# A value product with 7 block products for 8, and the norm moved to ScalarE, in a fused attention and gated-unit kernel

## Chip, cores, metric

One core of one Trainium2 chip. The time is device microseconds (us) of one execution on that core.

## The reference

```python
kv  = einsum('bhsd,bhse->bhde', k, v)          # b=8, h=8, s=576, d=64
o   = einsum('bhsd,bhde->bhse', q, kv)
o   = o / sqrt(mean(o*o, axis=-1) + 1e-6) * g_norm
x   = o as (8, 576, 512)                       # heads side by side
pre = sum over 5 taps of conv_w[tap] * x moved by 4 - tap tokens (zeros before the start)
out = ((sigmoid(pre) * (x @ w_val)) @ w_out)   # w_val, w_out 512 x 512
```

The three weights come as float64 and are narrowed by the kernel; the rest is float32.

## The kernel before

A batch is 576 tokens: four chunks of 128 and one of 64. For each chunk, TensorE makes `raw` (the attention output), then the norm follows, x is turned, gates and value product are made from it, and the output product closes the batch. The parts that matter here (cut):

```python
BANKS = {"kv": 1, "raw": 2, "tp": 2, "mm": 3}                 # PSUM banks by use
xTs = [const.tile([P, NK, SX], FP32, name=f"xT{i}") for i in range(3)]

def square(b, c):                      # ScalarE, all 8 heads of a chunk at once
    nc.scalar.activation(out=sq[:, 0:n, 0:D], in_=raw..., func=AF.Square)
def sums(b, c):                        # VectorE: the 8 head sums at once
    nc.vector.reduce_sum(out=ss[:, 0:n], in_=st["sq", b, c][:, 0:n], axis=AX.X)
def powers(b, c):                      # GpSimd: ss ** -0.5
def normalise(b, c):                   # VectorE: raw * rt, all 8 heads at once
    nc.vector.tensor_tensor(out=x..., in0=raw..., in1=rt....broadcast_to((P, n, D)), op=ALU.mult)

def val_product(b, jt, n):             # TensorE: 4 products of 128 rows for each block of 288 tokens
    for kc in range(NK):
        nc.tensor.matmul(val[:], wval[:, kc, jt * P:(jt + 1) * P],
            xTs[b % 3][:, kc, HALO + n * SV:HALO + (n + 1) * SV], start=(kc == 0), stop=(kc == NK - 1))
def keep_val(b, jt, n):                # ScalarE: one copy out of PSUM
    nc.scalar.copy(out=gv[:, jt, first:first + SV], in_=st["val", b, jt, n][:])
```

The output product already uses the 2x2 scheme with 7 block products (`fast_product`), with 2 copies and 5 additions for each pair of chunks (`fast_keep`).

**How the order comes about.** Each engine executes its own list of instructions in one fixed order (in the traces of the change and of the six experiments that keep its order, PE's 2113 records come in the same sequence, whatever their times), and the program makes that order itself: every step is entered with the engine, an *assumed duration*, a *wanted time*, what it needs, and the buffers it takes and frees; a planner then lists the steps by the earliest start it computes. A table of shifts, fitted by whoever wrote the kernel, corrects the wanted times.

```python
class Planner:
    HOP = 0.24                         # us from one engine to another
    def add(self, engine, time, want, fn, *args, needs=(), gives=(), takes=(), frees=(), ...):
        want += SHIFTS.get(fn.__name__, {}).get(which..., 0.0)
    def order(self):                   # always the step with the least (start, want)
...
plan.add("ACT", 0.52 * part, t + 1.0, square, b, c, needs=[("raw", b, c)], gives=[("sq", key)], ...)
plan.add("DVE", 0.6 * part, t + 4.2, normalise, b, c, needs=[("raw", b, c), ("rt", key)], ...)
```

## Time and profile before

| | before |
|---|---|
| time, median of 3 runs | 342.95 us (339.98 to 343.47) |
| span of the profiled run, granted clock | 339.4 us, 0.995 |
| TensorE (PE) / VectorE (DVE) / ScalarE (ACT) busy | 315.1 / 270.4 / 139.4 us |
| PE idle: first 82 us, 82 to 320, after 320 | 15.9, 3.2, 5.3 us |

The prediction below shows the page of this kernel and its main groups. Here is the busy time by stretch of the kernel before, in two stretches; the columns are the stretch, its length, PE, PE weight loads, DVE, ACT and GpSimd (busy us and instructions), granted clock, DMA share, GB/s:

```profile
0.00:82.00 82.00, 66.08 (x658) 54.84 (x659) 62.04 (x134) 52.52 (x113) 31.81 (x30) 0.98 1.00 274
82.00:320.00 238.00, 234.85 (x1450) 189.67 (x1449) 203.97 (x353) 85.21 (x177) 108.22 (x148) 1.00 0.51 133
```

In the middle PE is busy 234.85 of 238 us, while ACT is busy 85.21.

"Busy" counts the time covered by matmul records, and a record reaches past the point where the next one could start (407 ns mean against a spacing of 242.5), so a late start of less than about 0.16 us is hidden in it. I therefore also took **pace and loss** from the starts of the matmul records in the trace: for each kind of record (same product and size) the 30th percentile of the distance to the next start is its pace (242 ns for 288 columns, 216 for 256); the sum of the paces is the time that PE needs, and whatever the distances exceed it by is loss: waits, dependence stalls and stretches at half clock. Before: pace 274.3 us, loss 53.4 us (31.6 in the first 82 us, 21.3 from 82 to 320, 0.5 after), of which a part are small products that sometimes start nearly together.

### The profile page before, as it was taken

To read this page: it belongs to the slowest core of one execution; us is meant where nothing else is said; L and a number is where in the kernel's file an instruction comes from. 1 tells how busy PE (TensorE), PEld (TensorE's weight loads), DVE (VectorE), ACT (ScalarE), POOL (GpSimd) and SP (SyncE) were. 2 spreads that over 40 slices of the span, in tenths; PEclk is the share of its full clock that TensorE was granted. 3 is DMA by queue.
4 is the path that set the end of the run, shared out by engine and by line. 5 is a ranking of instruction groups with operands and counts; after the bars stand their busy time and mean duration, and the time that the engine had idled before them with its cause. 6 is when DMAs were issued, how large, how long until landed. Compare 5 with 4: busy or idle time off the path is not lost.

```text
span 339.4 us, 6185 instructions
## 1 busy us (share of the span) xinstructions
PE 315.1 (93%) x2161; PEld 254.7 (75%) x2161; DVE 270.4 (80%) x496; ACT 139.4 (41%) x293; POOL 140.0 (41%) x178
## 2 busy tenths in 40 slices
PE   0858999999999999999999999999999999999794
PEld 0747777878778877788778888778878876878681
DVE  4607999989999799896999899789956997297620
ACT  5528983873134253235134533172215322353010
POOL 3007314784356642683365585601717458000000
PEclk9998999999999999999999999999999999999999
DMA  6999979997077979787793165365333215220223
GB/s 165 287 329 306 320 219 299 250 315 168 3 178 196 244 233 280 187 236 207 206 256 86 32 154 157 71 182 144 79 89 85 64 31 129 58 63 2 62 62 93
DMA packets 46012, 55.35 MB, mean 163 GB/s; under 512 B 15754, under 2 KB 36254, under 8 KB 45982
## 3 DMA queue, kind: packets, MB, share of 16 engines
q1 hardware_dynamic: 42750, 48.67, 52.7%
q0 software_dynamic: 3072, 6.30, 8.3%
q8 instruction: 17, 0.28, 0.4%
q14 instruction: 13, 0.11, 0.1%
q10 hardware_dynamic: 160, 0.00, 0.0%
HBM read 39.21 MB, written 9.44 MB: 143 GB/s over the span
## 4 chain that ended last, share of the span: by engine, by line
PE 77%; DVE 8%; DMA 8%; ACT 3%; SPq 2%; issue 1%; POOL 1%; DVEq 0%
PE val L567 34%; PE ac L639 15%; PE b L639 11%; PE raw L469 8%; DMA q<-in_q_dram 5%; PE kv L392 4%; DMA k<-in_k_dram 2%; PE out L587 2%; PE qTps L430 2%; DVE gate L555 2%; PE xTps L515 1%; DVE sums L622 1%; DVE gv L580 1%; DMA out_dram<-ot 1%; DVE ss L491 1%
## 5 line engine op out<-in xcount | busy, mean ns | idle before, releaser
L567 PE MATMUL val<-xT,wval 128*128 128x288 f32 x512 | 129.5, 407 | 0.5 <-ACT gv L576 0.5
L567 PEld LDWEIGHTS val<-xT,wval 128*128 128x128 f32 x512 | 95.8, 190 | 26.9 <-issue 1.5
L497 POOL TENSOR_TENSOR rt<-ss,mhalf 128x8 f32<-128x8 f32 (+1 forms) x40 | 66.5, 1668 | 114.7 <-DVE ss L491 114.4
L555 DVE SCALAR_TENSOR_TENSOR gate<-xT,cwT,gate 128x576 f32<-128x576 f32 x128 | 97.4, 808 | 1.9 <-ACT gate L549 1.9
L538 POOL DMA_DIRECT2D xT<-y x96 | 52.9, 557 | 18.1 <-issue 6.5
L576 ACT COPY gv<-val 128x288 f32<-128x288 f32 x64 | 25.3, 395 | 69.3 <-PE val L567 69.1
L469 PEld LDWEIGHTS raw<-kvbd,qT 128*128 128x128 f32 (+1 forms) x320 | 36.8, 187 | 5.0 <-issue 1.9
L469 PE MATMUL raw<-kvbd,qT 128*128 128x128 f32 (+1 forms) x320 | 40.1, 286 | 0.0
L491 DVE TENSOR_REDUCE ss<-sq 128x8 f32<-128x520 f32 (+1 forms) x40 | 25.0, 630 | 17.5 <-ACT sq L483 17.5
L639 PE MATMUL b<-wsum,sums 128*128 128x256 f32 x128 | 33.6, 385 | 3.1 <-DVE sums L622 2.7
L639 PE MATMUL ac<-wout,gv 128*128 128x256 f32 x128 | 33.6, 385 | 0.2 <-DVE ot L662 0.2
L483 ACT ACTIVATE sq<-raw 128x512 f32<-128x512 f32 (+1 forms) x40 | 22.0, 553 | 24.0 <-PE raw L469 23.9
L639 PEld LDWEIGHTS b<-wsum,sums 128*128 128x128 f32 x128 | 23.1, 190 | 7.7 <-DVE sums L622 2.3
L504 DVE TENSOR_TENSOR x<-raw,rt 128x512 f32<-128x512 f32 (+1 forms) x40 | 24.9, 627 | 3.0 <-POOL rt L497 2.7
L639 PEld LDWEIGHTS ac<-wout,gv 128*128 128x128 f32 x128 | 23.4, 190 | 4.7 <-DVE ot L662 1.1
L562 ACT ACTIVATE gate<-gate 128x576 f32<-128x576 f32 x32 | 21.6, 684 | 11.8 <-DVE gate L555 11.4
L580 DVE TENSOR_TENSOR gv<-gv,gate 128x576 f32<-128x576 f32 x32 | 24.0, 749 | 2.6 <-ACT gv L576 1.9
L545 POOL COPY xT<-xT 128x124 f32<-128x124 f32 x32 | 18.7, 622 | 13.5 <-DMA xT<-y 13.5
L549 ACT ACTIVATE gate<-xT,cwT 128x576 f32<-128x576 f32 x32 | 22.2, 765 | 2.3 <-DMA xT<-y 2.2
L392 PEld LDWEIGHTS kv<-v,k 128*64 128x64 f32 x512 | 17.8, 138 | 6.5 <-issue 5.7
L392 PE MATMUL kv<-v,k 128*64 128x64 f32 x512 | 20.4, 225 | 1.9 <-DMA v<-in_v_dram 1.9
L655 ACT COPY ot<-ac 128x256 f32<-128x256 f32 x16 | 6.0, 372 | 35.6 <-PE ac L639 30.1
(78 smaller groups left out, 335.1 us busy)
## 6 DMA issues: line engine op xcount, KB each, us to landing
q<-in_q_dram SPq DMA_DIRECT2D x96, 140.0 KB, 4.6
out_dram<-ot SPq DMA_DIRECT2D x144, 64.0 KB, 1.8
k<-in_k_dram SPq DMA_DIRECT2D x16, 512.0 KB, 8.0
v<-in_v_dram SPq DMA_DIRECT2D x16, 512.0 KB, 7.3
xT<-y POOLq DMA_DIRECT2D x96, 64.0 KB, 2.7
w_wval<-in_moe_w_val_dram SPq DMA_DIRECT2D x4, 512.0 KB, 7.0
q<-in_q_dram SPq DMA_DIRECT2D x4, 512.0 KB, 8.7
w_wout<-in_moe_w_out_dram SPq DMA_DIRECT2D x4, 512.0 KB, 8.6
```

The source lines that it names most:

```text
L392: nc.tensor.matmul(kvp[r * D:(r + 1) * D, hp, :], st["k", b, half][:, h, j, :] if j < NJ else kl[:, 2 * hp + r, :], st["v", b, half][:, h, ...
L469: nc.tensor.matmul(raw[row * m:(row + 1) * m, col * P:(col + 1) * P], st["qT", b][:, hp, c * P:c * P + m], kv_bd[b % 2][:, hp, :], start=T ...
L491: nc.vector.reduce_sum(out=ss[:, 0:n], in_=st["sq", b, c][:, 0:n], axis=AX.X)
L497: nc.gpsimd.tensor_tensor(out=rt[:, 0:n], in0=st["ss", b, c][:, 0:n], in1=mhalf[:, 0:n], op=ALU.pow)
L504: nc.vector.tensor_tensor(out=x[:, 0:n * D].rearrange("p (h e) -> p h e", h=n), in0=st["raw", b, c][:, 0:n * D].rearrange("p (h e) -> p h ...
L538: nc.gpsimd.dma_start(out=xTs[b % 3][i * TB:(i + 1) * TB, :, first:first + P], in_=y[a * TB:(a + 1) * TB, i])
L549: nc.scalar.activation(out=gate[:], in_=xTs[b % 3][:, jt, HALO:SX], func=AF.Copy, scale=cwT[:, K - 1, jt:jt + 1])
L555: nc.vector.scalar_tensor_tensor(out=gate[:], in0=xTs[b % 3][:, jt, tap * TB:tap * TB + S], scalar=cwT[:, tap, jt:jt + 1], in1=gate[:], op ...
L567: nc.tensor.matmul(val[:], wval[:, kc, jt * P:(jt + 1) * P], xTs[b % 3][:, kc, HALO + n * SV:HALO + (n + 1) * SV], start=(kc == 0), stop=( ...
L576: nc.scalar.copy(out=gv[:, jt, first:first + SV], in_=st["val", b, jt, n][:])
L580: nc.vector.tensor_tensor(out=both, in0=both, in1=st["gate", b, jt][:], op=ALU.mult)
L639: nc.tensor.matmul(st[bank, i, p], tokens()[:, k], weights_[:, k], start=(n < 2 and k == 0), stop=(k == NK // 2 - 1), skip_group_check=True)
```

## The change

Its intent: PE sets the time, so the value product of batches 2 to 7 is made with 7 block products instead of 8. The sums and differences that this needs cost VectorE time, so the norm of those batches goes from VectorE to ScalarE, head by head. The output product's additions fall from 5 to 3. The order is replanned with a new table of shifts. The core of the diff (cut at "..."):

```diff
+    ACT_NORM = range(2, B)
+    ACT_SUMS = range(2, B)
+    FAST_VAL = range(2, B)
+    GATES = 3                                              # 4 gate tiles before
-    BANKS = {"kv": 1, "raw": 2, "tp": 2, "mm": 3}
+    BANKS = {"kv": 1, "raw": 2, "tp": 1, "mm": 4}
-    xTs = [... for i in range(3)]
+    xTs = [... for i in range(2)]
+    junk = const.tile([P, D], FP32, name="junk")
...
     def square(b, c):
+        if b in ACT_SUMS:
+            for h in range(n):
+                nc.scalar.activation(
+                    out=junk[:], in_=st["raw", b, c][:, h * D:(h + 1) * D], func=AF.Square,
+                    accum_out=ss[:, h:h + 1])
+            return
...
     def normalise(b, c):
+        if b in ACT_NORM:
+            for h in range(n):
+                cols = slice(h * D, (h + 1) * D)
+                nc.scalar.activation(out=x[:, cols], in_=st["raw", b, c][:, cols], func=AF.Copy,
+                    scale=st["rt", b, c][:, h:h + 1])
+            return
...
+    def val_fast(b, mj, n):            # n = 0..6, banks a, c, a, b, a, c, a
+        for k in range(NK // 2):
+            nc.tensor.matmul(st[bank, "val", b, mj][:], weights_[:, k], tokens()[:, k], ...)
+    def val_keep(b, mj, n):            # copies on ScalarE for n = 0, 1, 2, 6, additions on VectorE for 3, 4, 5
...
     def fast_keep(i, p, n):            # output product: 4 copies + 3 additions, 2 + 5 before
...
-            plan.add("ACT", 0.52 * part, t + 1.0, square, ...)
+                plan.add("ACT", 1.4 * part, t + 1.0, square, ...)
-            plan.add("DVE", 0.6 * part, t + 4.2, normalise, ...)
+            plan.add("ACT" if b in ACT_NORM else "DVE", (1.0 if b in ACT_NORM else 0.6) * part, t + 4.2, normalise, ...)
-    SHIFTS = {...}
+    SHIFTS = {...}                     # all new
```

The two assumed durations: 1.4 us for a block of 8 squares with sums, 1.0 us for a block of 8 multiplications.

## The prediction

> **What bounds the kernel now.** I read the page's busy shares first, then busy time by stretch, then TensorE's timeline, then the groups by form.
>
> ```profile
> PE 315.1 (93%) x2161; PEld 254.7 (75%) x2161; DVE 270.4 (80%) x496; ACT 139.4 (41%) x293; POOL 140.0 (41%) x178
> ...
> PE   0858999999999999999999999999999999999794
> ...
> DVE  4607999989999799896999899789956997297620
> ACT  5528983873134253235134533172215322353010
> ```
>
> TensorE (PE) is full in all slices but the first four and the last three; more than half of ScalarE's (ACT) time is free. The busy time by stretch has, after the stretch and its length, PE, PEld, VectorE (DVE), ACT and GpSimd (POOL):
>
> ```profile
> 0.00:20.00 20.00, 8.58 (x121) 7.49 (x121) 9.05 (x38) 10.07 (x24) 2.68 (x10) 1.00 0.94 246
> 20.00:34.00 14.00, 10.20 (x120) 9.22 (x121) 6.79 (x13) 8.42 (x19) 6.53 (x5) 0.88 1.12 309
> ...
> 82.00:300.00 218.00, 216.72 (x1372) 175.02 (x1371) 187.93 (x328) 79.17 (x164) 108.22 (x148) 1.00 0.55 141
> 300.00:339.40 39.40, 32.27 (x134) 24.81 (x133) 20.39 (x36) 7.74 (x17) 0.00 (x0) 1.00 0.20 51
> ```
>
> From 82 to 300 us PE lacks 1.3 us of 218. Of its 24.3 us of idle time in all, 15.2 lie in the first 34 us, where the DMA share is about 1, and 7.1 after 300 us. So in the middle only less PE work helps; DVE (188 of 218, 86%) is the second bound, close behind. PE busy is time covered by modelled matmul records, so I checked it by spacing. In the PE timeline, the value product and what follows it:
>
> ```profile
> 119.20 13.75 PE L567 MATMUL val<-xT,wval 128*128 128x288 f32 x56
> 132.78 1.03 PE L639 MATMUL ac<-wout,gv 128*128 128x256 f32 x4
> 133.64 1.03 PE L639 MATMUL b<-wsum,sums 128*128 128x256 f32 x4
> ...
> 318.96 1.13 PE L639 MATMUL b<-wsum,sums 128*128 128x256 f32 x4 [1.87 <-DVE sums L622]
> ```
>
> 56 records take 132.78 - 119.20 = 13.58 us, **0.2425 us each**, without a gap; four records of 256 columns take 0.86. This is the array's own pace, not a wait. The last line is the one large hole before the tail: after the last gate, two token sums. The groups by form that the change touches (mean ns of one after the comma):
>
> ```profile
> L567 PE MATMUL val<-xT,wval 128*128 128x288 f32 x512 | 129.5, 407 | 0.5 <-ACT gv L576 0.5
> ...
> L580 DVE TENSOR_TENSOR gv<-gv,gate 128x576 f32<-128x576 f32 x32 | 24.0, 749 | 2.6 <-ACT gv L576 1.9 <-ACT gate L562 0.6
> ...
> L491 DVE TENSOR_REDUCE ss<-sq 128x8 f32<-128x520 f32 x32 | 21.7, 683 | 5.9 <-ACT sq L483 5.9
> ...
> L504 DVE TENSOR_TENSOR x<-raw,rt 128x512 f32<-128x512 f32 x32 | 21.6, 679 | 0.8 <-POOL rt L497 0.5
> ...
> L483 ACT ACTIVATE sq<-raw 128x512 f32<-128x512 f32 x32 | 18.9, 596 | 18.7 <-PE raw L469 18.6
> ```
>
> **What the Trainium skill says.** (1) "TensorE: Matmul & The Clock Gate", section "Back-to-back issue gap": a warm matmul of N columns takes N/2.4 + 2.5 ns. The trace agrees for fp32 if each record streams its columns twice: 2 x 288/2.4 + 2.5 = 242.5 ns, as measured. So PE time here is proportional to the records, and one product in eight is one eighth of the value time. (2) "ScalarE: Activation LUTs", section "What ACT_TABLE_LOAD costs": 186 ns + 0.833 ns an element with immediates, about 93 ns more for a per-partition pointer, with about 93 ns of overlap between neighbours. In the trace a 256-column copy out of PSUM takes 370 ns and a 288-column one 395 (0.78 ns an element); two 280-column copies in a row start 0.27 us apart, so about 0.04 us is fixed, less than the page gives. (3) "Perfetto Trace Analysis", section "Optimizing Scalar/DVE Operations": each operation has a fixed data-access cost, so grouping helps and splitting hurts; it also says that moving work to ScalarE may help where DVE is saturated. The change does both. (4) "PSUM — Partial Sum Buffer", section "The four PSUM rules": GpSimd cannot touch PSUM, so the norm can only go to ScalarE if DVE is to lose it.
>
> **The change, part by part.**
>
> PE: the value product of one batch is 64 records now (512 over 8 batches) = 64 x 0.2425 = 15.52 us. After: 2 column pairs x 7 products x 2 blocks x 2 records = 56 records = 13.58 us. Saved 1.94 us a batch, **11.6 us over batches 2 to 7**, on the engine that sets the time. The output product keeps its 7 products and 256-column records: no change. PE busy becomes 315.1 - 11.6 = 303.5 us.
>
> DVE: removed per changed batch: sums 4 x 0.683 + 0.418 = 3.15 us, normalise 4 x 0.679 + 0.42 = 3.14. Added per batch: four differences of x over 576 columns, at the 0.749 of L580, 3.0 us; six additions of 288 columns, each 0.417 (the 256-column one) + 32/0.96 ns = 0.45, so 2.7. Net -0.6 a batch, -3.5 over six. Block additions of the output fall from 5 to 3 for each of 16 pairs of chunks: 32 x 0.42 = -13.4. Once: four sums of w_val, +2.7. In all **-14 us**, DVE to about 256: it stays near 85% in a shorter middle, so it neither leads nor frees much.
>
> ACT: a batch has four chunks of 8 heads and one of 4, so 4.5 chunks' worth of squares become 4.5 x 8 = 36 head-wide squares with a sum, and 36 head-wide multiplications with a pointer scale are new. Spaced by 64 x 0.833 + 40 = 93 ns, plus 93 for a pointer, a block of eight is 0.75 to 1.4 us for squares (the page gives no price for the sum; the program plans 1.4) and 1.0 to 1.5 us for the norm. I choose 2.4 us for both, against 0.55 now: 4.5 x 1.85 = 8.3 us a batch, 50 over six. Output copies go from 2 to 4 per pair: 32 x 0.33 = 10.6. ACT rises from 139 to about **200 us** (60%): not a bound, but evacuations of PSUM that PE waits for now stand behind blocks of 1 to 1.5 us.
>
> POOL gets 40 tiny additions, off the path.
>
> Waits that arise: in the new value product, products 3, 5 and 7 continue a bank that was copied out in the middle of its accumulation, with only one other product (4 x 0.2425 = 0.97 us) in between. The timeline shows such a round trip near the end, for the output product: its product ends at 325.97 us, the addition that reads the bank starts at 326.22 and takes 0.42, and with an estimated 0.1 back that makes 0.77. With 288 columns 0.8, so it fits in 0.97 if the engine is free, and not if it stands in a 0.7 us gate tap or a block of squares. There are 2 x 3 x 6 = 36 such places. Were a fifth of them late by 0.5 us, that is 3.6 us; the planner fills some with other products. I book **+3 us**. A single transpose bank (2 before) touches only batches 0 and 1: **+1**. At the end, the first output product after the last gate needs one token sum and not two, 0.7 of the 1.87 us hole of PE; with the free raw banks for the last outputs: **-1**.
>
> Sum: 342.95 - 11.6 + 3 + 1 - 1 = 334.3. The replanning was fitted to this program and may win back some of the 15 us of the start; I take off 0.8 and predict **333.5 us**.
>
> **Rivals.** (a) The saving is whole and replanning gives more: PE packed as before, start shortened by 3 us. For: the old middle lost 1.3 us with the same kind of tight places in the output product. It gives 329. (b) ACT's blocks delay the copies and PE gets new holes of 6 to 10 us: for it, ACT's record count rises by some 430 small ones, and each takes its turn in order; against it, ACT keeps 40% free and the norm is off the PE path. It gives 338 to 341. (c) Fewer buffers bind: two x tiles for three, three gates for four. The gate chain (16 taps of 0.76 us a batch) then starts later and DVE, at 85%, becomes the bound; 338 to 345. Against: a batch lasts some 36 us and its x is wanted for about one and a half of these.
>
> **Range and chances.** Rival (a) sets the low end, **328**; (b) the high end, **340**, as (c) seems less likely. Faster by over 2% needs less than 336.1 us, which is 2.6 above my centre: **0.71**. Within 2%: **0.26**. Slower by over 2% would need all the saving lost and 7 us more: **0.03**.
>
> **What would show it right or wrong.** Value records: 128 of the old kind and 336 new ones at the same 0.2425 spacing, PE busy near 303.5; DVE near 256; ACT near 200, with blocks of eight in 1.0 to 1.5 us. In the middle PE idle should be 3 to 6 us, mostly put down to ACT or DVE evacuations of the value banks. If ACT is above 230, its block cost is wrong; if PE idles for gate or x tiles, rival (c) is right; if PE's idle time in the first 34 us moves by more than 3 us, replanning and not the product has made part of the result.

## The result, and the profile after

| | before | after |
|---|---|---|
| time, median | 343.21 us (4 runs, 339.98 to 343.98) | 370.47 us (4 runs, 369.94 to 370.61) |
| profiled run: span, clock | 339.4, 0.995 | 368.0, 0.974 |
| PE / DVE / ACT busy | 315.1 / 270.4 / 139.4 | 320.6 / 262.1 / 241.1 |
| PE idle: first 82 us, 82 to 320, rest | 15.9, 3.2, 5.3 | 16.5, 25.4, 5.6 |
| PE pace + loss | 274.3 + 53.4 | 263.0 + 95.0 |

The ratio is 1.081 (95% interval 1.074 to 1.088): **slower by 8.1%**, far outside the predicted range. Here and below a ratio is the mean time of one kernel's fast runs over the mean of the other's in the same rounds, so it is not quite the ratio of the medians. All runs of this table are fast.

The page of the kernel after, busy shares and the slices that changed:

```profile
PE 320.6 (87%) x2113; PEld 251.2 (68%) x2113; DVE 262.1 (71%) x462; ACT 241.1 (66%) x943; POOL 151.7 (41%) x218
...
PE   3675999896989898999879988988979899999994
...
ACT  3475767689989887588986888274489943343321
```

ACT has 943 instructions for 293 and 241 us of work for 139. PE is no longer full in the middle: from the eighth to the thirty-second slice, thirteen of 25 show 6 to 8 tenths. By stretch, same columns as before:

```profile
0.00:82.00 82.00, 65.55 (x638) 53.05 (x639) 52.25 (x112) 51.05 (x143) 28.86 (x44) 0.98 0.98 264
82.00:320.00 238.00, 212.59 (x1300) 165.19 (x1299) 181.97 (x303) 176.07 (x770) 122.86 (x175) 0.97 0.49 131
```

In the middle PE falls from 234.85 to 212.59 us, ACT rises from 85.21 to 176.07 (74% of the stretch). The groups by form, ACT's blocks and the two products behind them (busy, mean ns of one | idle just before, and what ended it):

```profile
L495 ACT ACTIVATE junk<-raw 128x64 f32<-128x64 f32 x216 | 49.0, 227 | 14.0 <-PE raw L480 7.9
...
L525 ACT ACTIVATE x<-raw,rt 128x64 f32<-128x64 f32 x216 | 47.7, 347 | 7.1 <-POOL rt L514 6.1 <-DVE y L554 1.0
L495 ACT ACTIVATION_READ_ACCUMULATOR junk<-raw 128x1 f32 x216 | 42.8, 198 | 0.0
...
L724 PE MATMUL a<-wsum,sums 128*128 128x256 f32 x128 | 35.4, 400 | 10.6 <-ACT ot L735 5.4 <-ACT ot L739 5.2
L641 PE MATMUL va<-xs,vsum 128*128 128x288 f32 x96 | 29.2, 428 | 7.5 <-ACT gv L650 7.2 <-ACT gv L654 0.3
```

Three things are to be seen. The square with an accumulator output is *two* instructions, the square and an accumulator read, 216 of each. The output product (`a`, L724), which I had booked as "no change", loses 10.6 us, the new value product 7.5. And both wait for ScalarE copies (L735, L739, L650). What such a copy stands behind, in the ACT timeline (start, length, instruction, in brackets the idle time before):

```profile
268.65 0.23 ACT L495 ACTIVATE junk<-raw 128x64 f32<-128x64 f32 x1 [0.46 <-PE raw L480]
268.78 0.20 ACT L495 ACTIVATION_READ_ACCUMULATOR junk<-raw 128x1 f32 x1
269.00 0.22 ACT L495 ACTIVATE junk<-raw 128x64 f32<-128x64 f32 x1
...
271.20 0.19 ACT L495 ACTIVATION_READ_ACCUMULATOR junk<-raw 128x1 f32 x1
271.30 0.36 ACT L735 COPY ot<-a 128x256 f32<-128x256 f32 x1
```

and what PE does meanwhile:

```profile
268.39 1.03 PE L724 MATMUL a<-wout,gv 128*128 128x256 f32 x4
269.26 1.03 PE L724 MATMUL cb<-wsum,sums 128*128 128x256 f32 x4
271.71 1.13 PE L724 MATMUL a<-wsum,sums 128*128 128x256 f32 x4 [1.43 <-ACT ot L735]
```

Product `a` is done at 269.4; the copy that its next use of the bank waits for (L735) starts only at 271.30, after eight squares that took 271.39 - 268.65 = **2.74 us**, and PE stands for 1.43 us. Squares start every 0.347 us (median of all), so a block is 8 x 0.347 = 2.8 us, not 1.4. A block of multiplications spaces its eight by 0.197 us: 7 x 0.197 + 0.36 = 1.74 us until the last one's end, not 1.0. In the ACT timeline, a block and a half of them in a row:

```profile
274.28 2.59 ACT L525 ACTIVATE x<-raw,rt 128x64 f32<-128x64 f32 x12
```

**The account.** Pace falls by 11.3 us: the saving that was intended is there in full (the value records alone 123.9 to 112.3). Loss rises by 41.6 us: +6.2 in the first 82 us, **+34.6 from 82 to 320**, +0.8 after. PE's first record comes 1.8 us earlier. -11.3 + 41.6 - 1.8 = +28.5; the span grew by 28.6. The lower clock is part of the loss: up to PE's last record, stretches at half clock add up to 17.1 us after and 3.4 before, so it takes at most (17.1 - 3.4) / 2 = 6.8 us, less where PE was idle anyway. Each of these stretches is 3.4 us long or a multiple, which agrees with the Trainium skill, "TensorE: Matmul & The Clock Gate", section "What's actually happening", where windows of about 3.4 us decide the rate; so some of the lower clock may itself follow from the holes.

### The profile page after: what moved, and what is told of

It reads as the page before. It is cut to its first block, busy times and chain, and to the rows that moved or that the text cites. A ratio compares the mean times of both kernels' runs of the same rounds, so it can differ in the third digit from the quotient of the medians.

```text
span 368.0 us, 6707 instructions
## 1 busy us (share of the span) xinstructions
PE 320.6 (87%) x2113; PEld 251.2 (68%) x2113; DVE 262.1 (71%) x462; ACT 241.1 (66%) x943; POOL 151.7 (41%) x218
## 5 line engine op out<-in xcount | busy, mean ns | idle before, releaser
L513 POOL TENSOR_SCALAR ss<-ss 128x8 f32<-128x8 f32 (+1 forms) x40 | 16.5, 414 | 131.2 <-ACT junk L495 84.6
L562 POOL DMA_DIRECT2D xT<-y x96 | 53.4, 562 | 22.6 <-issue 14.5
L495 ACT ACTIVATE junk<-raw 128x64 f32<-128x64 f32 x216 | 49.0, 227 | 14.0 <-PE raw L480 7.9
L525 ACT ACTIVATE x<-raw,rt 128x64 f32<-128x64 f32 x216 | 47.7, 347 | 7.1 <-POOL rt L514 6.1
L724 PE MATMUL a<-wsum,sums 128*128 128x256 f32 x128 | 35.4, 400 | 10.6 <-ACT ot L735 5.4
L495 ACT ACTIVATION_READ_ACCUMULATOR junk<-raw 128x1 f32 x216 | 42.8, 198 | 0.0
L641 PE MATMUL va<-xs,vsum 128*128 128x288 f32 x96 | 29.2, 428 | 7.5 <-ACT gv L650 7.2
L724 PEld LDWEIGHTS a<-wsum,sums 128*128 128x128 f32 x128 | 23.3, 194 | 17.6 <-ACT ot L735 7.6
L591 PE MATMUL val<-xT,wval 128*128 128x288 f32 x128 | 33.9, 412 | 0.0
L591 PEld LDWEIGHTS val<-xT,wval 128*128 128x128 f32 x128 | 23.4, 190 | 6.5 <-issue 1.0
L641 PEld LDWEIGHTS va<-xs,vsum 128*128 128x128 f32 x96 | 17.9, 195 | 14.4 <-ACT gv L650 9.7
L586 ACT ACTIVATE gate<-gate 128x576 f32<-128x576 f32 x32 | 22.3, 708 | 5.9 <-DVE gate L579 5.8
```

The lines of the kernel that those rows point to most:

```text
L495: nc.scalar.activation(out=junk[:], in_=st["raw", b, c][:, h * D:(h + 1) * D], func=AF.Square, accum_out=ss[:, h:h + 1])
L525: nc.scalar.activation(out=x[:, cols], in_=st["raw", b, c][:, cols], func=AF.Copy, scale=st["rt", b, c][:, h:h + 1])
L562: nc.gpsimd.dma_start(out=xTs[b % 2][i * TB:(i + 1) * TB, :, first:first + P], in_=y[a * TB:(a + 1) * TB, i])
L591: nc.tensor.matmul(val[:], wval[:, kc, jt * P:(jt + 1) * P], xTs[b % 2][:, kc, HALO + n * SV:HALO + (n + 1) * SV], start=(kc == 0), stop=( ...
L641: nc.tensor.matmul(st[bank, "val", b, mj][:], weights_[:, k], tokens()[:, k], start=(n in (0, 1, 3) and k == 0), stop=(k == NK // 2 - 1), ...
L724: nc.tensor.matmul(st[bank, i, p], tokens()[:, k], weights_[:, k], start=(n < 2 and k == 0), stop=(k == NK // 2 - 1), skip_group_check=True)
```

## The experiments

The theory at the outset (T): ScalarE's blocks are longer than the order assumes, and copies that PE waits for stand behind them. Rivals: (R1) the new value product's own round trips through a bank; (R2) fewer buffers (one transpose bank for two, two x tiles for three, three gates for four); (R3) ScalarE simply has too much work, whatever the order.

### Undoing one part at a time: e1 to e4

```diff
e1  -ACT_NORM = range(2, B)   +ACT_NORM = ()      -ACT_SUMS = range(2, B)   +ACT_SUMS = ()
e2                                                -ACT_SUMS = range(2, B)   +ACT_SUMS = ()
e3  -ACT_NORM = range(2, B)   +ACT_NORM = ()
e4  -FAST_VAL = range(2, B)   +FAST_VAL = ()
```

In e1 and e2 the full-size squares use the ring of the weights' scratch for batches 2 to 7, as there was no room for another.

> The changed kernel with squares (one full-width instruction), sums and multiplication of the norm back where they were (sums and multiplication on VectorE); the value product with 7 products, the smaller buffers and the new order of requests stay. Theory A (ScalarE's long blocks of head-wide instructions delay the copies out of PSUM that TensorE waits for): ScalarE falls from 241 to about 155 us busy, TensorE idle from 47 to under 30 us, time 335 to 348 us, with VectorE near 300 us as the next bound. Theory B (the value product's own banks, one product between a bank's stop and its continuation, stall TensorE even with a free ScalarE): stays at 358 to 370 us, TensorE idle over 40 us. Theory C (fewer x tiles, gates and transpose banks): stays over 358 us too, but with TensorE waiting on x, gates or transposes.

> Only the sums of squares go back to VectorE (full-width square on ScalarE); the multiplication by the norm stays on ScalarE as 8 head-wide instructions. Theory A: ScalarE loses 92 us of squares and accumulator reads and gains about 16, so about 165 us; time 340 to 350 us. Theories B and C: over 358 us.

> Only the multiplication by the norm goes back to VectorE; the head-wide squares with sums stay on ScalarE. Theory A: ScalarE at about 193 us, the 2.8 us blocks of squares remain, time 350 to 362 us, worse than the run with the sums back. Theories B and C: over 360 us.

> The value product of all batches in its old form (8 products for 8, one copy per bank), everything else of the change kept: norm on ScalarE, 3 gates, 2 x tiles, 4 product banks. TensorE has 11.6 us more work. Theory A: ScalarE stays near 241 us and the time at 362 to 380 us. Theory B: TensorE's waits on the value banks go and the time falls to 340 to 352 us. Theory C: over 360 us.

| | time, median | ratio to before | ACT busy | pace + loss |
|---|---|---|---|---|
| after | 370.47 | 1.081 | 241.1 | 263.0 + 95.0 |
| e1: norm and sums on VectorE | 386.12 | 1.125 [1.119, 1.131] | 153.2 | 263.1 + 109.3 |
| e2: sums on VectorE | 385.25 | 1.124 [1.119, 1.130] | 194.7 | 263.0 + 110.1 |
| e3: norm on VectorE | 386.56 | 1.129 [1.123, 1.135] | 200.4 | 263.0 + 111.1 |
| e4: old value product | 379.74 | 1.108 [1.103, 1.114] | 241.2 | 274.6 + 91.9 |

All three undone norms are *slower* than the change, which no theory had expected. (One of e1's four runs, 390.98 us, counts as slow; it is in the median, not in the ratio.) The PE waits of e1 (what is waited for; total us, times, longest) point to the reason:

```profile
PE cb L724 <- DVE sums L701: 10.1, 4, 5.9
PE raw L480 <- DVE x L529: 6.3, 2, 3.8
```

Single waits of 5.9 and 3.8 us for VectorE steps are far longer than the 0.7 us of such a step; I read them as the cost not of an operation but of its place in the list, which e9 below bears out: when a part is undone, the planner orders *everything* anew, with shifts that were fitted to the other program. So e1 to e3 say nothing of the norm's cost, and that was a mistake in my design. e4 says one thing: its loss is 91.9 us, nearly that of the change, though there is no new value product in it, and its pace is 11.6 us more. The loss does not need the new product, against R1, with the reservation that e4 too was reordered. From here on I kept the order of the change and altered durations only.

### Shorter blocks in the same order: e5, e6, e7

Two heads in one instruction, with results that are **wrong**; the plan's assumed durations and so the order of all steps are untouched. In e5 and e6 the squares' sums are written into constant tiles, and in e6 an odd head takes the factor of its even neighbour.

```diff
-            for h in range(n):                          # square: e5, e6
+            for h in range(0, n, 2):
-                    in_=st["raw", b, c][:, h * D:(h + 1) * D], func=AF.Square,
+                    in_=st["raw", b, c][:, h * D:(h + 2) * D], func=AF.Square,
-            for h in range(n):                          # normalise: e5, e7
-                cols = slice(h * D, (h + 1) * D)
+            for h in range(0, n, 2):
+                cols = slice(h * D, (h + 2) * D)
```

> Same order of instructions as the changed kernel on every engine; only the head-wide instructions of ScalarE are done for two heads at once (4 squares with sums and 4 multiplications per chunk instead of 8 and 8; the norm is then taken over two heads, so the result is wrong on purpose). From the spacings of the changed kernel's trace, 0.345 us per square with its accumulator read and 0.219 per multiplication, plus 0.053 for the 64 further columns, a block is 1.6 and 1.1 us, close to the 1.4 and 1.0 us with which the order was planned, where the changed kernel's blocks take 2.76 and 1.75. Theory A2 (the order is made for blocks of 1.4 and 1.0 us, and the true blocks hold back the copies out of PSUM): time 334 to 343 us, TensorE idle below 28 us. Theory B (the value product's banks): over 360 us, as the banks are unchanged. Theory C (fewer buffers): over 360 us.

> As before it, but only the squares are paired (block 1.6 us for 2.76); the multiplications stay at 8. Wrong result on purpose. Theory A2, with the plan's order held and these durations put in: 343 to 351 us. Theories B and C: over 360 us.

> Only the multiplications are paired (block 1.1 us for 1.75); the squares with sums stay at 8. Wrong result on purpose. Theory A2, by the same estimate: 355 to 363 us. Theories B and C: over 363 us.

| | time, median | ratio to before | ACT busy |
|---|---|---|---|
| e5, both paired | 341.44 | 0.997 [0.991, 1.002] | 200.0 |
| e6, squares paired | 347.49 | 1.016 [1.010, 1.021] | 214.4 |
| e7, multiplications paired | 364.12 (two of its four runs count as slow, 364.99 and 365.80; the fast ones are 359.50 and 363.24) | 1.056 [1.046, 1.065] | not used, the profiled run is one of the slow ones |

With the blocks shortened the same order takes 29 us less, back to the time of before. Squares alone give 23 of it. (e7 was expected at 355 to 363 us; its slower fast run lies just above.) The group of paired squares of e5, and its middle by stretch:

```profile
L500 ACT ACTIVATE junk<-raw 128x128 f32<-128x128 f32 x108 | 30.1, 279 | 17.1 <-PE raw L484 14.5
...
L500 ACT ACTIVATION_READ_ACCUMULATOR junk<-raw 128x1 f32 x108 | 21.2, 197 | 0.0
```

```profile
82.00:320.00 238.00, 232.11 (x1425) 184.22 (x1425) 205.60 (x345) 147.95 (x490) 123.50 (x175) 1.00 0.53 137
```

A pair takes 0.40 us in the timeline, so a block is 1.6 us, near the planned 1.4, and four paired multiplications take 1.14, near 1.0. PE's busy time in the middle is back at 232.11 of 238 (212.59 in the change). This shows T: the **lengths of ScalarE's blocks in the order given** make most of the loss (95.0 us in the change, 66.5 here, 53.4 before). R1 falls: the new value product is in e5 as it was. R3 needs one more look, as e5 also took 41 us of work off ScalarE.

The planner's own account says the same. Keeping the change's order and counting with 2.76 and 1.75 us for the blocks, where the program assumed 1.4 and 1.0, moves the end of the plan from 335.7 to 369.8 us (370.47 measured); with 2.76 alone it is 357, with 1.75 alone 345. With the block lengths of e5 it is 337.0 (341.44 measured), of e6 346.8 (347.49), of e7 358.2 (359.5 and 363.2). It is a model, not a measurement, but in this fixed order it is wrong by 1 to 5 us where the effect is 29. (In the orders searched anew below it is further off: 2, 11, 7 and 8 us too early in e8, e9, e15 and e16.)

### Telling the plan the truth: e8, e9

```diff
e8  -"ACT", 1.4 * part, t + 1.0, square          +"ACT", 2.76 * part, t + 1.0, square
    -(1.0 if b in ACT_NORM else 0.6) * part      +(1.75 if b in ACT_NORM else 0.6) * part
e9  -ACT_NORM = range(2, B)                      +ACT_NORM = ()
    -ACT_SUMS = range(2, B)                      +ACT_SUMS = ()
both  SHIFTS = {...}                             # searched at random for the shortest plan
```

> The changed kernel with all its instructions, but the order is made anew for the true durations (blocks of squares 2.76 us, of multiplications 1.75; the requested times searched again for these). The plan then ends at 357 us by its own account, where it gave 336 for the durations assumed. Theory A2 in the strong form (only the order is wrong; ScalarE at 241 us has time enough): 330 to 345 us. Theory A3 (with true durations ScalarE's work itself costs time, whatever the order): 352 to 364 us, TensorE idle near 35 us.

> The value product with 7 products and the new buffers, but the norm on VectorE as before the change (right results), in an order searched anew for this division of the work; the plan ends at 340.6 us. If the first run with the norm back was slow only because its order was not made for it: 336 to 348 us. If VectorE, with about 292 us of work, or the value product's banks cost the time whatever the order: over 355 us.

e8 took 359.14 us (1.052 [1.044, 1.060]; plan 357), e9 351.15 us (1.027 [1.021, 1.033]; plan 340.6). True durations in the plan win back 11 us of 27, not all: with blocks of 2.76 us no order that I found keeps PE fed. Whether the rest is the length of a block or the sum of ScalarE's work, e8 does not tell. e9, the norm back on VectorE and *replanned*, is 35 us faster than e1, the same operations with the misfitted order. That is the size of the error in e1. (e9 was expected at 336 to 348 us, or over 355; it is in neither range.) Both have a lower clock (0.963 and 0.966) than before.

### Why a block of squares takes 2.8 us: e10, e13, e14

Mean lengths do not add up to it: a square is 227 ns and an accumulator read 198, but in the timeline above the read begins 0.13 us after its square's start, while the next square begins 0.22 us after the read's. In the trace the semaphore fields of each square show a wait on ScalarE's own semaphore, which the accumulator read before it raises. The source has no such wait. The one thing that both touch is `junk`, the 64-column scratch that all squares write. Two theories: the accumulator read itself is slow (then it is part of the operation's price), or the wait is (then another slice of scratch removes it). e10 drops the accumulator output, results wrong, and leaves the common scratch; e13 and e14 leave the accumulator and give neighbouring squares different slices, **with right results**. The order is the change's in all three.

```diff
e10 -   out=junk[:], in_=st["raw", b, c][:, h * D:(h + 1) * D], func=AF.Square, accum_out=ss[:, h:h + 1])
    +   out=junk[:, 0:D], in_=st["raw", b, c][:, h * D:(h + 1) * D], func=AF.Square)   # the last one: 1 column, into a constant ss
e13 -junk = const.tile([P, D], FP32, name="junk")      +junk = const.tile([P, 2 * D], FP32, name="junk")
    -   out=junk[:], ...                               +   out=junk[:, h % 2 * D:(h % 2 + 1) * D], ...
e14                                                    +junk = const.tile([P, 4 * D], bfloat16, name="junk")
                                                       +   out=junk[:, h % 4 * D:(h % 4 + 1) * D], ...
```

> The changed kernel in its own order; the head-wide squares stay separate instructions, but without the accumulator output, so that the accumulator reads are not there (the sums are then not formed: wrong result on purpose). If the term that my sum missed is the accumulator read (0.2 us each, 216 of them, between the squares of the trace): a block of squares falls from 2.76 to 0.9-1.1 us, below the 1.4 us that the order was planned for; with the multiplications still at 1.75 us the time is 341 to 349 us. If the squares themselves are what is dear: over 358 us.

> The changed kernel in its own order, right results; the thrown-away output of the head-wide squares alternates between two 64-column slices of the junk tile, where all eight squares of a block write one slice. In the trace of the changed kernel every square after the first carries a wait on ScalarE's own semaphore that the accumulator read before it raises. Theory D (this wait for the own previous write, through the shared junk slice, is what makes a square with its read 0.345 us and not the 0.175 that the order was planned for): the spacing falls to 0.17-0.25 us, a block to 1.4-2.0 us, and the time to 342-353 us. Theory E (square and accumulator read are that long by themselves): the spacing stays at 0.33-0.35 us and the time within 2 us of 370 us.

> As the run before it, with four slices (of half width in bytes, bf16, which fit beside the rest). Theory D: as fast as with two slices or up to 3 us faster, as the wait then looks four squares back. Theory E: as the changed kernel.

| | spacing of squares | time, median | ratio to before |
|---|---|---|---|
| after | 0.347 | 370.47 | 1.081 |
| e10, no accumulator, one scratch | 0.255 | 349.78 | 1.023 [1.018, 1.028] |
| e13, accumulator, two slices | 0.197 | 349.32 | 1.018 [1.014, 1.022] |
| e14, accumulator, four slices | 0.197 | 349.73 | 1.020 [1.015, 1.025] |

The ACT timeline of e13, two squares of a block:

```profile
261.86 0.22 ACT L495 ACTIVATE junk<-raw 128x64 f32<-128x64 f32 x1
261.98 0.19 ACT L495 ACTIVATION_READ_ACCUMULATOR junk<-raw 128x1 f32 x1
262.07 0.21 ACT L495 ACTIVATE junk<-raw 128x64 f32<-128x64 f32 x1
262.17 0.20 ACT L495 ACTIVATION_READ_ACCUMULATOR junk<-raw 128x1 f32 x1
```

The single instructions are no shorter (over all of e13 a square is 253 ns and a read 237, where they were 227 and 198), but the next square now starts 0.09 us after the read does, where it took 0.22. So the accumulator read takes about 0.09 us of ScalarE's list (squares with neither read nor common scratch were not run), and the **wait through the common scratch costs 0.347 - 0.197 = 0.15 us a square**, 1.2 us a block, more than the planned length of a block of multiplications. e10 shows it from the other side: without the accumulator, but with one scratch, squares still follow each other only every 0.255, seven of them in

```profile
266.75 1.75 ACT L500 ACTIVATE junk<-raw 128x64 f32<-128x64 f32 x7
268.40 0.17 ACT L500 ACTIVATE ssc<-raw 128x1 f32<-128x1 f32 x1
```

Four slices give nothing over two. A block of e13 is 8 x 0.197 = 1.6 us. (e10's block was expected to take 0.9 to 1.1 us and takes 1.8: its theory, that the read is the missing term, is the smaller part of the truth. It is no faster than e13 in all, as its block is the longer one.)

An edit of two lines thus takes 21 us off the change, with right results, and the account says where: the middle of e13,

```profile
82.00:320.00 238.00, 226.90 (x1393) 179.21 (x1391) 199.77 (x332) 166.36 (x787) 122.29 (x175) 0.99 0.50 135
```

has PE busy 226.90 for 212.59, and the loss there is 34.5 us for 55.9, so 21.4 us less (up to 5.1 of them because half-clock stretches in the middle fall from 13.7 to 3.4 us). R3 in its plain form does not fit either: e13 leaves every instruction in place and has ScalarE still at 221.6 us, 64% of its span (241.1 and 66% in the change), yet most of the excess over the kernel before is gone. But e13 too takes some 28 us of waiting (189 spacings of 0.15) out of ScalarE's list, so it does not separate the length of a block from the sum of the work. What does so in part is e8: the same work in another order is 11 us faster. For the rest of the 27 us R3 is not excluded.

### What is left: e11, e12, e15, e16

e5 shows that with blocks near their planned lengths the change only equals the kernel before, though its pace is 11.3 us shorter. In its account the loss is 13.0 us higher than before: 6.8 in the first 82 us, 6.0 in the middle, 0.2 after. The buffers (R2) were tried alone in the kernel *before*, with its order kept:

```diff
e11  only the bank, the plan still counts two:   -"tp": 2   +"tp": 1
e12  -xTs = [... for i in range(3)], xTs[b % 3]  +xTs = [... for i in range(2)], xTs[b % 2]
```

> The kernel before in its own order, with one PSUM bank for transposes where it has two (the change takes one away to give the products four). Theory C for the start: the transposes of batches 0 and 1 wait for each copy, 345 to 352 us, the loss before 82 us of the span. If the bank is not missed: within 1 us of the kernel before.

> The kernel before in its own order, with two x tiles where it has three, as in the change. Theory C: some us slower, with TensorE or VectorE waiting for x. If two are enough: within 2 us of the kernel before.

e12 took 342.71 us (1.002 [0.997, 1.007]): two x tiles cost nothing. Three gates in the order of before leave a circular wait (by the planner; there is no run of it), so that could not be tried. e11 took 354.49 us (1.037 [1.031, 1.042]); expected were 345 to 352. Its loss is 12.7 us higher, and the first 82 us alone have 13.5 more (45.1 for 31.6; the middle is 2.9 lower, the rest 2.1 higher). Its PE waits in these 82 us:

```profile
PE qTps L430 <- ACT qT L459: 4.8, 4, 2.3
...
PE qTps L430 <- ACT xT L522: 2.1, 3, 0.7
```

With two banks, in the same stretch, PE waited 0.4 us for ScalarE's copies out of them. So **one transpose bank costs some 12 us in the first 82** of an order that was planned for two, where I had booked 1. In e5 the same kind of wait is there, again in the first 82 us:

```profile
PE xTps L544 <- DVE x L534: 5.2, 4, 2.5
...
PE qTps L445 <- ACT qT L474: 4.2, 3, 2.5
```

The first is a wait for x itself, the second for the bank. How much of e5's 6.8 us is the bank in the *change's* order stays open: a version with a second bank for batches 0 and 1 was not run.

e15 and e16 put the mended scratch and its true lengths into the plan and search the shifts anew, twice, for right results:

```diff
-junk [P, D], out=junk[:]                         +junk [P, 2 * D], out=junk[:, h % 2 * D:(h % 2 + 1) * D]
-"ACT", 1.4 * part, ... square                    +"ACT", 1.6 * part, ... square
-(1.0 if b in ACT_NORM else 0.6) * part           +(1.6 if b in ACT_NORM else 0.6) * part
-SHIFTS = {...}                                   +SHIFTS = {...}       # searched; e15 and e16 differ only here
```

> The whole change with the two scratch slices and right results, in an order searched anew for blocks of 1.6 us (squares) and 1.6 us (multiplications); the plan ends at 337.8 us by its own account, 343.8 for the kernel before. If the shared scratch slice and the durations assumed for it are all that stood against the saving of 11.6 us: 333 to 341 us. If the half-clock windows and the start, which the plan doesn't know, take their part as in the orders searched before (plan 340.6, measured 351): 343 to 350 us.

> The same in a second order from the search, plan 338.0 us: within 4 us of the first, or the order matters beyond what the plan knows.

e15: 344.82 us over 6 runs, 1.006 [1.002, 1.011]; e16: 346.34, 1.013 [1.007, 1.020]. e15 is the best version of the change with right results, and it does not beat the kernel before. By stretch:

```profile
0.00:82.00 82.00, 63.92 (x618) 52.97 (x619) 56.34 (x118) 48.92 (x126) 27.37 (x42) 0.94 0.97 269
82.00:320.00 238.00, 232.23 (x1425) 183.19 (x1424) 199.20 (x331) 169.27 (x808) 127.55 (x177) 1.00 0.49 132
```

Its pace is 11.1 us below that of before, its loss 17.2 above: 9.6 in the first 82 us (PE does 618 products there, 658 before, at a clock of 0.94 for 0.98), 6.8 in the middle, 0.7 after. In both e5 and e15, then, more of the saving goes in the start than in the middle, though the first record of the new value product comes only at 135 us (in e5 two of its four sums of weights, 1.5 us of VectorE, do lie in the start).

## Why the prediction was wrong, by its steps

- **"one product in eight is one eighth of the value time ... 11.6 us over batches 2 to 7": right.** 128 old and 336 new value records at the same 242 ns; the value pace fell from 123.9 to 112.3 us. "PE busy becomes 315.1 - 11.6 = 303.5" was nevertheless wrong (320.6), since busy time also holds short delays and half-clock stretches; I had treated it as a constant of the program.
- **"DVE to about 256": right in direction** (262.1, so 8 us less and not 14; the new additions of 288 columns took the 0.45 us that were put down for them).
- **"I choose 2.4 us for both" blocks: the step that failed.** Measured 2.76 + 1.58 to 1.75, about 4.4 us. The 2.4 lies just above the middle of my ranges (1.75 to 2.9 together) and is exactly the program's own 1.4 + 1.0, so it checked nothing. It missed two terms: 0.15 us of waiting between neighbouring squares, because all write one scratch (e13), 1.2 us a block; and the accumulator read, with which a block of squares is still 1.6 us when that wait is gone. The count of ACT's records shows the reads: I said 430 more, 650 came, 216 of them reads. ACT became 241, not 200; the prediction's own sign, "If ACT is above 230, its block cost is wrong", fired.
- **"I book +3 us" for waits: the term of the sum that was mis-sized**, and with it "+1" for the transpose bank. The loss grew by 41.6 us. Of the 34.6 in the middle, 21.4 go with the scratch (after to e13, same order), 7.2 more with pairing both blocks (e13 to e5, loss 34.5 to 27.3), and 6.0 remain. I counted 36 places in the *value* product and called the output product "no change"; it waits 10.6 us for its copies (L735, L739), more than the value product's 7.5. Its copies stand in the same list, and the change had doubled them.
- **Rival (b), "ACT's blocks delay the copies", had the mechanism right and the size wrong**: 6 to 10 us said, 22.3 us more PE idle time measured in the middle. What I held against it, "ACT keeps 40% free", was the error of thought: a free share over the whole run says nothing of how long a copy waits behind a block; here ACT is free 26% of the middle and a copy stood 1.9 us behind eight squares.
- **"The replanning was fitted to this program": believed without a check.** The diff shows the assumed lengths, 1.4 and 1.0 us; the order was fitted to these. My own ranges (0.75 to 1.4, and 1.0 to 1.5) had these lengths at an end each, the 1.0 at the low one, and I did not ask what a plan with wrong lengths does. e5 shows what the plan is worth where its lengths nearly hold: 29 us. The start was not shortened: PE's idle time in the first 34 us went from 15.2 to 14.8.
- **Rival (c)**, fewer buffers: two x tiles cost nothing (e12). The transpose bank cost not "+1" but 12 us in the order of before (e11); its part in the change's order is open. Gates were not tried.

## What to carry to other kernels

Before work is moved to an engine as many small instructions, ask what each of them writes: a scratch that nobody reads tied neighbours together here, and a second slice of it was worth 21 us. Where a program orders its instructions by assumed durations, check these durations in the trace before anything else, and when undoing a part for an experiment keep the order, or the experiment measures the order. An engine's free share did not bound the wait behind it here; look at the length of its longest uninterrupted block, against the slack of whoever waits.

## What the Trainium skill lacked or had wrong

- "ScalarE: Activation LUTs", section "What it computes", says that an ACTIVATE can give an accumulator output. It does not say that this is a second instruction or what it costs: here 216 squares came with 216 accumulator reads, about 0.09 us each in ScalarE's list where nothing waits (a square and its read every 0.197 us in e13). Two instructions are described for VectorE, in "VectorE: DVE Perf Modes", section "Two Vector instructions with no wait between them".
- No page gives the price of a ScalarE instruction that waits for its neighbour on the same engine through an output that both write: 0.347 us from square to square, for 0.197 with two slices (e13). "VectorE: DVE Perf Modes", section "The DRAIN you can't avoid", finds for VectorE that a semaphore between neighbours "costs nothing extra here"; on ScalarE it cost 0.15 us.
- "ScalarE: Activation LUTs", section "What ACT_TABLE_LOAD costs": its figures give 186 + 64 x 0.833 + 93 - 93 = 239 ns from start to start for a 64-column ACTIVATE with a pointer scale (an estimate from the page); here such instructions, reading PSUM, started 197 ns apart. The section does not say for which memory its figures hold, so this may be a gap and not an error.
